# Transposing attention probabilities by DMA instead of on TensorE, in a fused attention and two-layer kernel

## The chip, the cores and the metric

The kernel runs on one core of a Trainium2 chip. The metric is the device time of one execution in microseconds, as the median of several runs. The kernel before takes 693.0 us.

The core's engines work side by side, each through its own queue of instructions in program order: TensorE (PE, with its weight loads shown apart as PEld), VectorE (DVE), ScalarE (ACT), GpSimd (POOL) and SyncE (SP), whose queue issues most of the DMA transfers here. An instruction that waits holds everything behind it on its own engine.

## The reference, cut to what matters

```python
scores = scale * np.matmul(q, k.transpose(0, 1, 3, 2))      # 4 batches, 8 heads, 576 positions, 64 wide
scores = np.where(masks, scores, -1e9)                      # window of 32, plain or dilated by 4
attn = np.exp(scores - np.max(scores, axis=-1, keepdims=True))
attn = attn / (np.sum(attn, axis=-1, keepdims=True) + 1e-09)
x = np.matmul(attn, v)                                      # then laid out as [2304 tokens, 512]
h = x @ w_in                                                # 512 -> 2048
x = (h - np.tanh(h)) @ w_out                                # 2048 -> 512
h2 = x @ w_in2                                              # 512 -> 1024, then h2 * softmax(h2), layer norm
out = ln @ w_out2                                           # 1024 -> 512
```

## The kernel before

**Units.** Attention is cut into 48 units of four blocks: each block is 96 queries against 128 keys. Eight units make the x of one group of 384 tokens; there are six groups. For each unit the scores go to PSUM (`qk_f32` for units below 20, `qk_half` twice for the others, which use split operands made by `prep_unit`). VectorE adds the mask and takes the row maximum (L337 and L340 for the split form) and writes the tile `p` of 96 x 4 x 128 float32 values. ScalarE applies the exponential in place (`sm_exp`, L348). `sm_norm` forms the reciprocal of the row sums on VectorE (L353, L354) and multiplies `p` by it on GpSimd (L356).

**The transpose.** The product with v needs the keys on the partitions. So `tr_pe` transposes the four blocks of `p` on TensorE against the identity into one PSUM tile (L363), and ScalarE copies this into the SBUF tile `pt` of 128 x 384 (L369). `pv_pe` multiplies two units' `pt` by v (L384); its evacuation writes x as a rounded part on ScalarE (L393) and a rest on VectorE (L395). PSUM tiles of attention come from the pool `a_ps`, which has two buffers. `p` has three buffers, `pt` five.

**The main stage.** Steps s = 0 to 95 are six groups by sixteen columns of the hidden layer. A step has two slots: in the first TensorE does the twelve matmuls of `mm1(s)` (L457), in the second the twelve of `mm2(s - 5)` (L484). The activation of `mm1(s)` is a chain of four: tanh on ScalarE (L465), subtraction on VectorE (L468, `sub`), rounding on ScalarE (L471, `hi`), rest on VectorE (L474, `lo`). The PSUM tiles of `mm1` have two buffers, so `mm1(s + 2)` needs `sub` of step s to be done.

**The order by hand.** `plan` hangs the work of the units of later groups into the slots. For unit u from 16 on, p = 4u - 41 is its first slot: the scores are multiplied in slots p and p + 1, the reciprocal and product come in slot p + 4, the transposes in slot p + 6, and the product with v for four units together, five slots after the transposes of the fourth one. A unit's round is thus four slots. In each slot a fixed order holds: the TensorE work, then the activation parts, the evacuations of the TensorE pieces of the slot before (`nxt`), and then the list `later` of the slot in the order of its registering.

**Loads.** All loads are issued from SP. While units 20 to 39 are worked on, the tile `qkr` of a unit is used first to bring in a piece of the second layer's weights (`sc_load`, L188), whose maximum is taken by `sc_max` (L208), and then for the unit's q and k (L179). `v` comes from L274.

**The last part.** The second layer (L748, L763 and on) uses DMA transposes already: `split_z` (L877) transposes a tile of 128 x 2048 float16 values, in two parts a and b, into `zt`.

Of the kernel before, what the change touches and what calls it, by code (L numbers as in the profile page):

```python
# [7 lines left out]
F32 = mybir.dt.float32  # L8
F32R = mybir.dt.float32r
I32 = mybir.dt.int32  # L10
F16 = mybir.dt.float16
BF16 = mybir.dt.bfloat16
U16 = mybir.dt.uint16
AF = mybir.ActivationFunctionType
ALU = mybir.AluOpType
# [9 lines left out]
NQ, NK = 96, 128  # L25
NU = 8
QC, KC = 4 * NQ, 4 * NK
# [13 lines left out]
def tile_kernel(ctx: ExitStack, tc: tile.TileContext, qk, vw, cst, w_in, w_out, w_in2, w_out2, g_ln, out):  # L41
    nc = tc.nc
    ctx.enter_context(tc.manual_schedule())

    const = ctx.enter_context(tc.tile_pool(name="const", bufs=1, side="left"))
# [12 lines left out]
    at_p = tc.alloc_tile_pool(name="at", bufs=2, side="right")  # L58
# [23 lines left out]
    ymx = const.tile([128, NG, KD], F32, name="ymx")  # L82
    ym = const.tile([128, NG], F32, name="ym")
    ysc = const.tile([128, NG // 2, 3, 3], F32, name="ysc")
    id16 = const.tile([128, 128], F16, name="id16")

# [76 lines left out]

    xt, un = {}, {}
    NFU = 20

    def new_qk(u):
        un[u] = dict(r=at_p.tile([128, QC + KC], F32, tag="qkr", name=f"qkr{u}"))  # L170

    def load_qk(u):
# [3 lines left out]
        elif u not in un:  # L176
            new_qk(u)
        n = 64 if u < NFU else 128
        nc.sync.dma_start(out=un[u]["r"][:n], in_=qk[u, :n])  # L179

    def sc_load(u, i):

        new_qk(u)
        r = un[u]["r"].bitcast(I32)
        k, q = divmod(i, 10)
        w = w_in2.rearrange("a b p n -> (a b) p n") if k else w_out2
        if q < NF2:
            nc.sync.dma_start(out=r, in_=w[q][:, 0:QC + KC])  # L188
        else:
            h = 4 * (q - NF2)  # L190
            nc.sync.dma_start(out=r[:, 0:512].rearrange("p (j n) -> p j n", j=4),
                              in_=w[h:h + 4].rearrange("j p n -> p j n")[:, :, QC + KC:])
# [84 lines left out]
    def load_unit(u):  # L277
        if u < NU * NG:
            load_qk(u)
            load_v(u)  # L280

    def prep_unit(u):
        if not NFU <= u < NU * NG:
            return []
        r = un[u]["r"]
        s = qs_p.tile([128, QC + 2 * KC], F32R, tag="qks", name=f"qks{u}")
        un[u]["s"] = s
        return [
            lambda: nc.scalar.copy(out=s[:, 0:QC + KC], in_=r),
            lambda: nc.vector.tensor_tensor(out=s[64:128, 0:QC], in0=r[64:128, 0:QC],  # L290
                                            in1=s[64:128, 0:QC].bitcast(F32), op=ALU.subtract),
            lambda: nc.vector.tensor_tensor(out=s[:, QC + KC:], in0=r[:, QC:],
                                            in1=s[:, QC:QC + KC].bitcast(F32), op=ALU.subtract),
        ]
# [7 lines left out]
    def qk_f32(u, pool, tag):  # L302

        d = un[u]
        new_p(u)
        ps = pool.tile([128, 512], F32, tag=tag, name=f"qkp{u}")[:NQ, 0:KC].rearrange("p (b k) -> p b k", b=4)
        for b in range(4):
            nc.tensor.matmul(ps[:, b], d["r"][:64, b * NQ:(b + 1) * NQ],  # L308
                             d["r"][:64, QC + b * NK:QC + (b + 1) * NK], start=True, stop=True)

        def then():
            for b in range(4):
                nc.vector.tensor_tensor_reduce(  # L313
                    out=d["p"][:, b], in0=ps[:, b], in1=masks[:, mask_of(u, b % 2)], op0=ALU.add, op1=ALU.min,
                    scale=-0.125, scalar=3.0e38, accum_out=d["nm"][:, b:b + 1])
        return then
# [28 lines left out]
    def sm_exp(u, bs=range(4)):  # L345
        d = un[u]
        for b in bs:
            nc.scalar.activation(out=d["p"][:, b], in_=d["p"][:, b], func=AF.Exp, scale=-1.0,  # L348
                                 bias=d["nm"][:, b:b + 1], accum_out=d["sm"][:, b:b + 1])

    def sm_norm(u):
        d = un[u]
        nc.vector.tensor_scalar(out=d["rs"], in0=d["sm"], scalar1=1e-9, scalar2=None, op0=ALU.add)  # L353
        nc.vector.reciprocal(out=d["rs"], in_=d["rs"])  # L354
        eng = nc.vector if u == NU - 1 else nc.gpsimd
        eng.tensor_tensor(out=d["p"], in0=d["p"],  # L356
                          in1=d["rs"].unsqueeze(2).to_broadcast([NQ, 4, NK]), op=ALU.mult)

    def tr_pe(u, pool, tag, eng="a"):
        d = un[u]  # L360
        ps = pool.tile([128, 512], F32, tag=tag, name=f"tp{u}")
        for b in range(4):
            nc.tensor.transpose(ps[:NK, b * NQ:(b + 1) * NQ], d["p"][:, b], ident[:NQ, :NQ])  # L363
        pt = at_p.tile([NK, QC], F32, tag="pt", name=f"pt{u}", bufs=5)
        d["pt"] = pt

        def then():
            if eng == "a":
                nc.scalar.copy(out=pt, in_=ps[:NK, 0:QC])  # L369
            else:  # L370
                nc.vector.tensor_copy(out=pt, in_=ps[:NK, 0:QC])
        return then

    def pv_pe(u, pool, tag):

        g, r = divmod(u, NU)
        hp = r // 2
        x = xt[g, hp] = x_ps[g % 2].tile([128, 2, G], F32R, tag=f"x{hp}", name=f"x{g}_{hp}")
        ps = pool.tile([128, 512], F32, tag=tag, name=f"pv{u}")[:, 0:G]
        for i in range(2):  # L380
            d = un.pop(u + i)
            for b in range(2):
                for h in range(2):
                    nc.tensor.matmul(ps[64 * h:64 * h + 64, (2 * i + b) * NQ:(2 * i + b + 1) * NQ], d["v"][:, b, h],  # L384
                                     d["pt"][:, (2 * h + b) * NQ:(2 * h + b + 1) * NQ], start=True, stop=True)
        sl, src = [x[:, i] for i in range(2)], ps
        if hp >= 2:
            sl = [a.rearrange("p (i r) -> p r i", r=DIL) for a in sl]
            src = ps.rearrange("p (r i) -> p r i", r=DIL)

        def then(parts="hl"):
            if "h" in parts:
                nc.scalar.copy(out=sl[0], in_=src)  # L393
            if "l" in parts:
                nc.vector.tensor_tensor(out=sl[1], in0=src, in1=sl[0].bitcast(F32), op=ALU.subtract)  # L395
        return then
# [50 lines left out]
    def at(slot, fn):  # L447
        later.setdefault(slot, []).append(fn)
# [54 lines left out]
    u0, u1 = NU, NU * NG  # L503
    preps = []

    def piece(slot, fn):
        todo.setdefault(slot, []).append(fn)

    def plan():


        ready = 0
        for u in range(u0, u1 + 2):
            p = 4 * u - 41 if u >= 2 * NU else (2, 6, 8, 12, 14, 16, 18, 20)[u - u0]
            q = p + 2 if u >= 2 * NU or u < u0 + 4 else p + 1
            if u < u1:
                at(p + 1, lambda u=u: preps.extend(prep_unit(u + 1)))
                for i in (1, 1, 2):
                    at(p + i, lambda: preps.pop(0)() if preps else None)
                if u < NFU:  # L520
                    piece(p, lambda u=u: qk_f32(u, a_ps, "at"))
                    at(p + 1, lambda u=u: sm_exp(u))
                    at(p + 2, lambda u=u: sm_norm(u))
                else:
                    piece(p, lambda u=u: qk_half(u, 0, a_ps, "at"))
                    at(p + 2, lambda u=u: sm_exp(u, (0, 1)))
                    piece(p + 1, lambda u=u: qk_half(u, 1, a_ps, "at"))
                    at(p + 3, lambda u=u: sm_exp(u, (2, 3)))
                    at(p + 4, lambda u=u: sm_norm(u))
                i = u - NFU  # L530
                if 0 <= i < 20:
                    at(p - 1, lambda u=u, i=i: sc_load(u + 2, i))
                    at(p + 1, lambda u=u, i=i: sc_max(u + 2, i))
                if i == 20:
                    at(p - 1, lambda u=u: new_qk(u + 2))
                    at(p - 1, lambda u=u: sc_rows(u + 2))
                    piece(p + 1, lambda: sc_pe(a_ps, "at"))
                at(p + 1, lambda u=u: load_unit(u + 2))
            if u0 <= u - 1 < u1:
                piece(q, lambda u=u: tr_pe(u - 1, a_ps, "at"))  # L540
            if u % 4 == 1 and u0 <= u - 5 < u1:
                for w in (u - 5, u - 3):
                    piece(q + 1, lambda w=w: pv_pe(w, a_ps, "at"))

    plan()


# [191 lines left out]
    p3 = ctx.enter_context(tc.tile_pool(name="p3", bufs=2, side="left", reuse_waits="tile"))  # L739
# [151 lines left out]
    def mm4(i, mid=None):  # L891
# [11 lines left out]
        nc.scalar.activation(out=o, in_=po, func=AF.Copy, scale=d["g"])  # L903
        nc.sync.dma_start(out=out[i * TT:(i + 1) * TT, :], in_=o)

    nc.gpsimd.tensor_copy(out=id16, in_=ident)
    y_rows(2)
    split_y(2, ("r", "s"))
# [126 lines left out]
```

## Time and profile before

| | |
|---|---|
| median of 3 runs | 693.0 us (691.96 to 693.55) |
| the profiled execution | 692.85 us, of which the trace's span is 691.1 us |
| TensorE busy | 671.4 us, 97% of the span |
| VectorE busy | 501.5 us, 73% |
| ScalarE busy | 384.3 us, 56% |
| GpSimd busy | 173.3 us, 25% |
| mean granted TensorE clock | 0.998 of full speed |

The span runs from the first to the last instruction of the trace; 1.75 us of the execution's time lie around it. Busy time is the time in which an engine has at least one instruction under way. Matmuls are pipelined: one starts before the one ahead of it has ended, so the time that a matmul costs is the distance between starts, not its own duration.

### The profile page before, as it was taken

How to read it: one execution, taken by the hardware profiler on the slowest of the kernel's cores; microseconds unless marked ns; L12 is line 12 of the kernel's file. 1: busy time of each engine (PE TensorE's matmuls, PEld its weight loads, DVE VectorE, ACT ScalarE, POOL GpSimd, SP SyncE). 2: the span in 40 equal slices, each digit the busy share in tenths (PEclk: the TensorE clock that was granted, in tenths of full speed). 3: DMA queues.
4: the chain of work that ended last, by engine and by line, in shares of the span. 5: the costliest groups of instructions: out<-in, count | busy, mean ns of one | idle time of the engine just before them, and what ended most of it. 6: DMA issues, size and time to landing. Idle time of an engine off the chain costs nothing. (4 is left out here: it accounts for less than half of the span.)

```text
span 691.1 us, 11384 instructions
## 1 busy us (share of the span) xinstructions
PE 671.4 (97%) x4010; PEld 558.3 (81%) x4010; DVE 501.5 (73%) x1251; ACT 384.3 (56%) x917; POOL 173.3 (25%) x174
## 2 busy tenths in 40 slices
PE   6988999999999999999999999999999999999997
PEld 5787999999999999999999999999964444444443
DVE  4987667468777876787767853489978888777752
ACT  5778876545554555555554543466736645555442
POOL 2312311101101110111110110246414666545410
PEclk9999999999999999999999999999999999999999
DMA  9975640233433334442322100463512464433243
GB/s 281 353 246 173 212 125 23 86 121 119 123 104 116 111 121 123 121 142 74 97 69 71 45 1 1 152 202 134 168 46 45 114 147 95 93 94 76 71 92 92
DMA packets 68009, 80.82 MB, mean 117 GB/s; under 512 B 36592, under 2 KB 52464, under 8 KB 67952
## 3 DMA queue, kind: packets, MB, share of 16 engines
q1 hardware_dynamic: 64784, 75.37, 37.6%
q10 hardware_dynamic: 3168, 4.72, 1.8%
q8 instruction: 32, 0.52, 0.3%
q14 instruction: 25, 0.20, 0.1%
HBM read 62.25 MB, written 9.44 MB: 104 GB/s over the span
## 5 line engine op out<-in xcount | busy, mean ns | idle before, releaser
L457 PE MATMUL h<-x,wi 128*128 128x384 f32 x1152 | 221.5, 342 | 1.2 <-DVE t L468 1.2
L484 PE MATMUL y<-gs,wo 128*128 128x384 f32 x1152 | 217.9, 339 | 0.0
L457 PEld LDWEIGHTS h<-x,wi 128*128 128x128 f32 x1152 | 199.4, 190 | 2.5 <-DVE t L468 1.4
L484 PEld LDWEIGHTS y<-gs,wo 128*128 128x128 f32 x1152 | 199.8, 189 | 1.8
L356 POOL TENSOR_TENSOR p<-p,rs 96x512 f32<-96x512 f32 x47 | 57.5, 1224 | 352.3 <-DVE rs L354 316.9
L474 DVE TENSOR_TENSOR gs<-t,gs 128x384 fp32r<-128x384 f32 x96 | 81.4, 848 | 24.3 <-ACT gs L471 24.2
L468 DVE TENSOR_TENSOR t<-h,t 128x384 f32<-128x384 f32 x96 | 53.0, 552 | 63.3 <-ACT t L465 63.2
L900 PE MATMUL po<-w2o_o,zt 128*128 128x512 f16 x432 | 94.9, 379 | 0.0
L465 ACT ACTIVATE t<-h 128x384 f32<-128x384 f32 x96 | 46.8, 488 | 83.3 <-PE h L457 80.0
L348 ACT ACTIVATE p<-p,nm 96x128 f32<-96x128 f32 x192 | 74.9, 392 | 21.3 <-DVE nm L313 21.0
L471 ACT CAST gs<-t 128x384 fp32r<-128x384 f32 x96 | 48.9, 509 | 63.6 <-DVE t L468 63.4
L900 PEld LDWEIGHTS <-zt 128*128 128x128 f16 x432 | 42.1, 98 | 51.1 <-DMA zt<-e 0.5
L748 PEld LDWEIGHTS <-yt 128*128 128x128 f16 x378 | 36.8, 98 | 47.0 <-issue 3.4
L823 ACT ACTIVATE e<-hn,sml 128x1024 f32<-128x1024 f32 x18 | 20.7, 1149 | 56.3 <-DVE sml L763 43.5
L748 PE MATMUL sp<-w2i_t,yt 128*128 128x512 f16 x216 | 48.6, 379 | 2.2 <-DVE u L786 2.2
L873 DVE SCALAR_TENSOR_TENSOR e<-hn,sml,e 128x1024 f16<-128x1024 f32 x18 | 25.6, 1426 | 19.6 <-ACT e L872 19.6
L748 PE MATMUL sp<-w2i_b,yt 128*128 128x512 f16 x162 | 37.9, 379 | 0.0
L308 PE MATMUL qkp<-qkr 64*96 64x128 f32 x160 | 29.5, 339 | 7.3 <-DMA qkr<-in_qk_dram 5.5
L348 ACT ACTIVATION_READ_ACCUMULATOR p<-p,nm 96x1 f32 x192 | 36.2, 188 | 0.0
L308 PEld LDWEIGHTS qkp<-qkr 64*96 64x96 f32 x160 | 24.1, 205 | 11.8 <-DMA qkr<-in_qk_dram 5.9
L395 DVE TENSOR_TENSOR x<-pv,x 128x384 fp32r<-128x384 f32 x24 | 16.2, 697 | 19.8 <-ACT x L393 19.4
L363 PE MATMUL tp<-cst_sb,p 96*128 96x96 f32 x192 | 27.0, 268 | 3.4 <-POOL p L356 2.4
(111 smaller groups left out, 826.2 us busy)
## 6 DMA issues: line engine op xcount, KB each, us to landing
qkr<-in_qk_dram SPq DMA_DIRECT2D x28, 448.0 KB, 3.4
raw_wi<-in_w_in_dram SPq DMA_DIRECT2D x16, 511.8 KB, 7.2
raw_wo<-in_w_out_dram SPq DMA_DIRECT2D x16, 511.8 KB, 7.1
v<-in_vw_dram SPq DMA_DIRECT2D x48, 128.0 KB, 3.4
y_dr<-ys ACTq DMA_DIRECT2D x6, 768.0 KB, 3.9
yr<-y_dr SPq DMA_DIRECT2D x9, 512.0 KB, 4.5
out_dram<-o SPq DMA_DIRECT2D x18, 256.0 KB, 2.9
qkr<-in_qk_dram SPq DMA_DIRECT2D x20, 224.0 KB, 5.2
```

The costliest lines, as they stand in the source:

```text
L308: nc.tensor.matmul(ps[:, b], d["r"][:64, b * NQ:(b + 1) * NQ], d["r"][:64, QC + b * NK:QC + (b + 1) * NK], start=True, stop=True)
L348: nc.scalar.activation(out=d["p"][:, b], in_=d["p"][:, b], func=AF.Exp, scale=-1.0, bias=d["nm"][:, b:b + 1], accum_out=d["sm"][:, b:b + 1])
L356: eng.tensor_tensor(out=d["p"], in0=d["p"], in1=d["rs"].unsqueeze(2).to_broadcast([NQ, 4, NK]), op=ALU.mult)
L363: nc.tensor.transpose(ps[:NK, b * NQ:(b + 1) * NQ], d["p"][:, b], ident[:NQ, :NQ])
L457: nc.tensor.matmul(ps, w[:, a, k * 128:(k + 1) * 128], xt[g, k][:, b], start=(n == 0), stop=(n == 3 * KD - 1))
L465: nc.scalar.activation(out=t, in_=ps, func=AF.Tanh)
L468: nc.vector.tensor_tensor(out=t, in0=ps, in1=t, op=ALU.subtract)
L471: nc.scalar.copy(out=gs[:, 0], in_=t)
L474: nc.vector.tensor_tensor(out=gs[:, 1], in0=t, in1=gs[:, 0].bitcast(F32), op=ALU.subtract)
L484: nc.tensor.matmul(yb[g][m], wo[c][:, a, m * 128:(m + 1) * 128], gs[:, b], start=(c == 0 and i == 0), stop=(c == NF - 1 and i == 2))
L748: nc.tensor.matmul(ps, y[:, a, blk, kk], w2i[w, kk][:, b], start=first and q == 0, stop=q == 5, skip_group_check=not first)
L900: nc.tensor.matmul(po, z[:, a, j], w2o[j][:, b], start=(q == 0), stop=(q == 3 * NF2 - 1))
```

## The change

For units 16 to 47 (`DT` = 16 is the first), TensorE does not transpose `p` any more.

- `sm_norm` divides the row sum by 2^14 in the instruction that adds 1e-9, so that `p` comes out 2^14 times as large.
- `p_new` takes a further tile of the tag `p` (three buffers, as before, now for two tiles a unit) and views it as float16.
- `p_hi`, in slot p + 5, copies `p` on ScalarE into the first half of it as float16; `p_lo`, in slot p + 6, writes `p` less that copy into the second half on VectorE, and issues a DMA transpose of the 96 x 1024 float16 values from SP into the new tile `ptt` (two buffers).
- `p_sum`, in slot p + 9, adds the two transposed parts on VectorE into `pt`, which has four buffers now.
- The evacuation in `pv_pe` takes the factor 2^14 out again: the ScalarE copy gets a scale, the VectorE subtraction becomes a multiply and subtract.
- The float16 identity `id16` moves from the constants into the pool of the last part, so its memory is reserved later.

```diff
+    DT = 2 * NU
...
     def sm_norm(u):
         d = un[u]
-        nc.vector.tensor_scalar(out=d["rs"], in0=d["sm"], scalar1=1e-9, scalar2=None, op0=ALU.add)
+        nc.vector.tensor_scalar(out=d["rs"], in0=d["sm"], scalar1=1e-9, scalar2=2.0 ** -14 if u >= DT else 1.0,
+                                op0=ALU.add, op1=ALU.mult)
...
+    def p_new(u):
+        un[u]["ab"] = at_p.tile([NQ, 4, NK], F32, tag="p", name=f"pab{u}", bufs=3).bitcast(F16).rearrange(
+            "p b (a k) -> p (b a k)", a=2)
+
+    def p_hi(u):
+        d = un[u]
+        nc.scalar.copy(out=d["ab"][:, 0:4 * NK], in_=d["p"].rearrange("p b k -> p (b k)"))
+
+    def p_lo(u):
+        d = un[u]
+        ab = d["ab"]
+        nc.vector.tensor_tensor(out=ab[:, 4 * NK:], in0=d["p"].rearrange("p b k -> p (b k)"), in1=ab[:, 0:4 * NK],
+                                op=ALU.subtract)
+        d["tt"] = at_p.tile([NK, 2, 4, NQ], F16, tag="ptt", name=f"ptt{u}")
+        nc.sync.dma_start_transpose(out=d["tt"].rearrange("p a b q -> p (a b) q"), in_=ab)
+
+    def p_sum(u):
+        d = un[u]
+        d["pt"] = at_p.tile([NK, QC], F32, tag="pt", name=f"pt{u}", bufs=4)
+        nc.vector.tensor_tensor(out=d["pt"].rearrange("p (b q) -> p b q", b=4), in0=d["tt"][:, 0], in1=d["tt"][:, 1],
+                                op=ALU.add)
...
-        pt = at_p.tile([NK, QC], F32, tag="pt", name=f"pt{u}", bufs=5)
+        pt = at_p.tile([NK, QC], F32, tag="pt", name=f"pt{u}", bufs=4)
...
         def then(parts="hl"):
+            if g * NU >= DT:
+                nc.scalar.activation(out=sl[0], in_=src, func=AF.Copy, scale=2.0 ** -14)
+                nc.vector.scalar_tensor_tensor(out=sl[1], in0=src, scalar=2.0 ** -14, in1=sl[0].bitcast(F32),
+                                               op0=ALU.mult, op1=ALU.subtract)
+                return
...
-            if u0 <= u - 1 < u1:
+            if DT <= u < u1:
+                for i, fn in ((3, p_new), (5, p_hi), (6, p_lo), (9, p_sum)):
+                    at(p + i, lambda u=u, fn=fn: fn(u))
+            if u0 <= u - 1 < min(u1, DT):
                 piece(q, lambda u=u: tr_pe(u - 1, a_ps, "at"))
```

## Rows read from the trace of the kernel before

**Rows 1.** The page, busy time, share of the span and instructions of each engine.
```profile
PE 671.4 (97%) x4010; PEld 558.3 (81%) x4010; DVE 501.5 (73%) x1251; ACT 384.3 (56%) x917; POOL 173.3 (25%) x174
```

**Rows 2.** Windows: stretch, its length, busy us of each engine, clock, DMA share, GB/s.
```profile
100.00:420.00 320.00, 320.00 (x2127) 313.93 (x2126) 228.56 (x658) 171.76 (x484) 35.27 (x34) 1.00 0.29 91
138.58:414.99 276.41, 276.41 (x1842) 272.17 (x1842) 203.46 (x585) 147.00 (x418) 30.24 (x30) 1.00 0.31 97
...
300.00:320.00 20.00, 20.00 (x145) 19.52 (x144) 16.98 (x49) 12.01 (x37) 2.08 (x2) 1.00 0.42 135
```

**Rows 3.** Timeline of TensorE, end of attention: start us, us, instruction.
```profile
410.82 2.24 PE L457 MATMUL h<-x,wi 128*128 128x384 f32 x12
412.90 2.24 PE L484 MATMUL y<-gs,wo 128*128 128x384 f32 x12
414.99 0.49 PE L363 MATMUL tp<-cst_sb,p 96*128 96x96 f32 x4
...
417.43 2.24 PE L484 MATMUL y<-gs,wo 128*128 128x384 f32 x12
```

**Rows 4.** Groups of instructions by line: count, busy us, mean ns of one, idle before.
```profile
L356 DVE TENSOR_TENSOR p<-p,rs 96x512 f32<-96x512 f32 x1 | 0.7, 689 | 0.0
...
L290 DVE TENSOR_TENSOR qks<-qkr,qks 64x384 fp32r<-64x384 f32 x28 | 15.6, 556 | 0.9
...
L369 ACT COPY pt<-tp 128x384 f32<-128x384 f32 x48 | 22.8, 474 | 5.0 <-PE tp L363 4.8
...
L289 ACT CAST qks<-qkr 128x896 fp32r<-128x896 f32 x28 | 26.2, 937 | 0.0
...
L363 PE MATMUL tp<-cst_sb,p 96*128 96x96 f32 x192 | 27.0, 268 | 3.4 <-POOL p L356 2.4 <-DVE p L356 0.9
```

**Rows 5.** Timeline of all engines, one round: start us, us, instruction, idle before.
```profile
251.34 0.50 PE L363 MATMUL tp<-cst_sb,p 96*128 96x96 f32 x4
...
251.96 0.33 SPq L188 DMA_DIRECT2D qkr<-in_w_in_dram  x1
...
254.57 0.56 DVE L468 TENSOR_TENSOR t<-h,t 128x384 f32<-128x384 f32 x1 [2.13 <-ACT t L465]
...
255.58 1.04 POOL L356 TENSOR_TENSOR p<-p,rs 96x512 f32<-96x512 f32 x1 [8.14 <-DVE rs L354]
255.58 0.94 ACT L289 CAST qks<-qkr 128x896 fp32r<-128x896 f32 x1
...
255.71 1.32 DVE L474 TENSOR_TENSOR gs<-t,gs 128x384 fp32r<-128x384 f32 x1 [0.30 <-ACT gs L471]
...
256.10 2.25 PE L457 MATMUL h<-x,wi 128*128 128x384 f32 x12
256.95 0.41 DVE L337 TENSOR_TENSOR p<-qkp,cst_sb 96x256 f32<-96x256 f32 x1
...
257.93 0.56 DVE L290 TENSOR_TENSOR qks<-qkr,qks 64x384 fp32r<-64x384 f32 x1
...
258.45 0.49 ACT L465 ACTIVATE t<-h 128x384 f32<-128x384 f32 x1 [1.94 <-PE h L457]
258.52 0.62 DVE L208 TENSOR_REDUCE mx<-qkr 128x1 f32<-128x448 bf16 x1
...
259.93 0.55 DVE L468 TENSOR_TENSOR t<-h,t 128x384 f32<-128x384 f32 x1
...
260.52 0.50 PE L363 MATMUL tp<-cst_sb,p 96*128 96x96 f32 x4
```

**Rows 6.** Timeline of TensorE, transposes of unit 19.
```profile
145.32 0.49 PE L363 MATMUL tp<-cst_sb,p 96*128 96x96 f32 x4
```

**Rows 7.** Instructions of tile zt: duration ns, min/median/max, and their landing.
```profile
L877 SPq DMA_TRANSPOSE zt<-e x16: 1696/1906/3652, 528.5 to 676.6; - x16
...
DMA to landing us min/median/max: 4.2/4.3/5.9
```

**Rows 8.** DMA from 528 to 534 us: busy tenths in 40 slices.
```profile
DMA  0000000000005999999999999999810000000000
```

More of the change, by code (lines that the diff above doesn't have):

```diff
@@ L84, in tile_kernel @@
     ysc = const.tile([128, NG // 2, 3, 3], F32, name="ysc")
-    id16 = const.tile([128, 128], F16, name="id16")
     wq, wld, wa, wf, wh = [], [], [], [], []
@@ L904, in mm4 @@
         nc.sync.dma_start(out=out[i * TT:(i + 1) * TT, :], in_=o)
+    id16 = p3.tile([128, 128], F16, name="id16", bufs=1)
     nc.gpsimd.tensor_copy(out=id16, in_=ident)
```

## The prediction

> **What bounds the kernel now.** I read the page first: TensorE is busy 97% of the span, VectorE 73% [rows 1]. Busy time alone doesn't prove a bound, so the windows come next. From 100 to 420 us, which holds all the work that is changed (the first changed unit's scores come at slot 23, just before 100 us), TensorE is busy 320.00 of 320 us at a granted clock of 1.00, VectorE 228.56, ScalarE 171.76, and the DMA engines 29% [rows 2]. The reader should see an engine without a gap beside one with 29% to spare. The timeline then shows that matmuls follow each other at their own pace: the twelve of one slot begin 2.08 us after the twelve of the slot before [rows 3], and nothing waits in between. So in this stage a matmul that goes away shortens the kernel by its pitch, as long as no other engine becomes the slowest. What comes behind 420 us depends on the stage's end and shifts with it.
>
> **What the change takes from TensorE.** It removes the four transposes of each of 32 units, 128 instructions. The groups give 268 ns for one [rows 4], which would make 34 us, but that counts overlapped time. The timeline has the price: from one `mm2` slot's start to the next `mm1` to the next `mm2`, slots without transposes take 2.08 us (410.82 to 412.90), and from the transposes at 414.99 past the following `mm1` to the next `mm2` at 417.43 it is 2.44 us [rows 3]. The difference, 0.36 us, is what four transposes cost with the switch of shapes. 32 x 0.36 = 11.4 us (unrounded 0.355).
>
> A round of four slots is 9.18 us now, from the transposes at 251.34 to those at 260.52 [rows 5], and would be 8.83. With the products with v and the group ends the average round is (414.99 - 145.32) / 28 = 9.63 us, from unit 19's transposes to unit 47's [rows 3, 6]; it would be 9.28.
>
> **What it adds to VectorE.** `p_lo` is a two-operand instruction on 96 x 512; the same shape on VectorE took 689 ns. `p_sum` has 384 elements a partition; L290 with as many took 556 ns [rows 4]. Together 1.25 us a unit. Neither operand mix (float16 with float32) is in the trace; the upper end is that each also meets GpSimd's product as `lo` does, which takes 1.32 us beside it [rows 5] against L290's 0.56, so 0.76 more each and 2.77 in all. The lower end is that either costs what its row shows and no more. I take 1.25, since GpSimd's one product a unit already slows one VectorE instruction and the new ones come later in the round. VectorE's demand was 203.46 of 276.41 us [rows 2], 7.09 per average round; it becomes 8.34 of 9.28, or 90%. It fits, with less reserve: around a group's end, where `y_max` comes in, VectorE is at 16.98 of 20 [rows 2], and 2.6 more makes 19.6 against 19.3 that the shorter rounds leave. That overrun is a queue, not yet a stall: the `sub` that ends at 255.13 is needed only by the `mm1` two steps on, behind the transposes at 260.52, over 5 us later [rows 5]. I allow 1 us in all for such places; bounds 0 and 5 us (eight dense rounds of 0.6). The factor in the evacuation leaves the number of instructions as it is: costed at nothing, hidden by VectorE's reserve, and at most a tenth of a microsecond in 16 places if not.
>
> **What it adds to ScalarE.** The copy `pt` of 474 ns goes, `p_hi` with 512 elements comes; between 474 ns for 384 and 937 for 896 [rows 4] that is about 0.59, so 0.12 more a unit, 4 us in all, on an engine busy 171.76 of 320 [rows 2]. More important is its place: `p_hi` waits for GpSimd's product, and behind it in ScalarE's queue stand the cast `qks` (L289) and the next tanh. In the round shown the product ends at 256.62; p_hi to 257.3, cast to 258.2. The tanh starts at 258.45 because its matmuls end only then [rows 5], so it isn't delayed. VectorE wants the cast for L290 at 257.93, but `p_sum` now stands ahead of it and moves that to 258.5. Cost nothing; if the product takes longer, VectorE waits for that in its 10% reserve.
>
> **What it adds to SP and the DMA engines.** 32 transposes of 96 x 1024 float16, 192 KB each, against the 512 KB of `zt`. The latter holds SP for 1.9 us and lands 4.3 us (4.2 to 5.9) after its issue [rows 7]. In one such transfer the DMA engines start 1.8 us into the window, 1.3 us after the issue at 528.5, and run for about 2.5 [rows 7, 8]. At three eighths of the bytes that is 0.95, and 1.3 + 0.95 + 0.5 for the end gives 2.8 us. Bounds: 2.8 and zt's longest, 5.9. I take 3, as the DMA engines are 29% busy; loads issued a slot earlier are mostly through. On SP, the next `sc_load` (251.96) is queued behind `p_lo` and the transpose, some 1 to 2 us later. It is read at 258.52 [rows 5]; with 4 us of transfer it still arrives in time. `load_qk` and `load_v` have a round to spare. POOL's queue gets no more instructions.
>
> **The new loop.** `p` still has three buffers, but a unit takes two. Unit u + 2's first VectorE write (L337) goes into unit u's float16 tile, so it must wait for unit u's DMA transpose. The loop of a round is: `p_lo`, landing, L337, and on VectorE everything up to the next `sub` and the next `p_lo`. From L337 at 256.95 to the end of `sub` at 260.48 is 3.53 us [rows 5]; with `p_sum` and `p_lo` 4.78. A landing of L us makes a loop of L + 4.78: 7.8 at L = 3, under the 8.83 of the shortest round. At zt's 4.3 it is 9.1, still under the average 9.28, the products with v giving the time back. `id16` and the smaller number of `pt` buffers cost nothing: the identity is first wanted in the last part, and `pt` of a unit is written after the product with v that frees it.
>
> A rule that speaks against the change: the Trainium skill, VectorE: DVE Perf Modes, section The three transpose paths, gives 390 ns for a 128 x 128 bf16 transpose on TensorE and 1309 ns by DMA. By these prices of the Trainium skill, an estimate, eight tiles one after another would land in 10.5 us and every round would last 15 us. The trace disagrees for tiles in one transfer: sixteen land together in 4.3 us [rows 7].
>
> **The sum.** The profiled execution is 692.85 us, its span 691.1. 692.85 - 11.4 + 1 = 682.5. The median shown, 693.0, is 0.15 above it, so 682.6.
>
> **The rivals.**
> *VectorE becomes the bound.* At the upper price of 2.77 us its demand is 9.86 a round against 9.28: 32 x 0.58 = 18.6 us back, 700 us. From 2.19 us on the gain shrinks, at 2.54 it is gone. For it: 90% busy in an engine that works in order, with new waits on ScalarE and DMA. Against it: it still waits 2.13 us for a tanh in the round shown [rows 5]. Halfway, with an extra wait of 1.2 us a round, the time is about 690.
> *The transposes land late (slower than before).* The place is L337's wait for the buffer of `p`. The loop equals today's average round of 9.63 at L = 4.85; above that the kernel is slower. At 5.9 it is 10.68, 1.05 us a round more, 32 x 1.05 = 34: 727 us. For it: zt reached 5.9, and loads share the queue. Against it: three eighths of the bytes. The prices of the Trainium skill (VectorE: DVE Perf Modes, The three transpose paths) would put the kernel in this case.
> *The cost of the transposes was hidden anyway.* If something else gave the pace, the time would stay at 693. Against it: 0.36 us more in every slot with transposes, without an idle TensorE [rows 2, 3].
>
> **How the numbers follow.** My forecast (680.5 to 686) gets 0.67; VectorE partly in the way (686 to 691.5) 0.12; no change 0.04; VectorE fully the bound 0.05; late transposes 0.12. The likeliest is 682.6. The range of 680.5 (11.4 taken and a little more) to 692 holds the first two and part of the third, 8 in 10; the late case would lie far outside. Differences below 0.2%, 1.4 us, can't be told from none. Faster: 0.79; same: 0.04; slower: 0.17.
>
> **What would show it.** In the changed profile: 128 fewer TensorE instructions, and 64 transposes left at L363; rounds of about 8.83 us without the product with v; `p_lo` near 0.69 and `p_sum` near 0.56 us, 32 each; VectorE near 268 of 309 us in the stage; DMA transposes of `ptt` landing in about 3 us; and no idle time of VectorE at the first write of `p`. Wrong, it would be: TensorE idle before `mm1` with `sub` as the releaser, VectorE idle behind the DMA of `ptt`, or landings of more than 4.5 us.

## The result and the profile after

The changed kernel takes 684.88 us, the median of four runs (683.13 to 686.35), against 692.93 us before (four runs, 691.96 to 693.55): a ratio of 0.9884 with a 95% interval of 0.9857 to 0.9911. It is 1.2% faster: the direction is as forecast, the time is inside the range of 680.5 to 692 and 2.3 us above the likeliest value of 682.6. The profiled execution took 683.13 us, its span 681.3.

The page's busy times answer to [rows 1]: 128 instructions of TensorE are gone, 64 of VectorE are new (`p_lo` and `p_sum`).

```profile
PE 661.0 (97%) x3882; PEld 547.9 (80%) x3882; DVE 532.6 (78%) x1315; ACT 386.3 (57%) x917; POOL 174.5 (26%) x174
```

The window that answers to [rows 2], with the columns told there, ends at 410 us now, since the work behind it moved forward by 9.7 us:

```profile
100.00:410.00 310.00, 309.99 (x2007) 304.03 (x2006) 260.80 (x723) 174.74 (x486) 36.37 (x34) 1.00 0.43 114
```

TensorE still has no gap, VectorE rose from 71% to 84%, and the DMA share from 0.29 to 0.43. So the bound of the stage is what it was. Rounds without the product with v are read from the timeline of TensorE, at the first scores (L328) of three units in a row:

```profile
206.55 0.40 PE L328 MATMUL qkp<-qks 128*96 128x256 f32 x2
...
215.36 0.40 PE L328 MATMUL qkp<-qks 128*96 128x256 f32 x2
...
224.17 0.40 PE L328 MATMUL qkp<-qks 128*96 128x256 f32 x2
```

They are 8.81 us apart; before it was 9.18 [rows 5], and 8.83 was forecast. The new instructions, by the tile that holds the two float16 parts (durations in ns as min/median/max, then first and last start):

```profile
L366 ACT CAST pab<-p x32: 612/619/623, 110.8 to 402.3; 96x512 f16<-96x512 f32 x32
L371 DVE TENSOR_TENSOR pab<-p,pab x32: 676/678/679, 115.8 to 404.8; 96x512 f16<-96x512 f32 x32
L374 SPq DMA_TRANSPOSE ptt<-pab x32: 1212/1213/2224, 116.6 to 405.5; - x32
its engine sat idle before it (us, times) until:
  POOL p L357: 23.4, 24
  DMA ptt<-pab: 8.0, 4
...
DMA to landing us min/median/max: 2.8/2.9/4.8
```

L366 is `p_hi`, L371 `p_lo`, L374 the transpose; `p_sum` (L379) has a median of 550 ns. The reader should see two things: a landing of 2.9 us, and that the instruction that waits for landings is `p_hi` on ScalarE, in four places (`p_sum` waits once, for 0.2 us).

**The stage gave 11.1 us, and 8.1 arrived.** From the first scores of slot 23 to the last product with v, the timelines of TensorE give 99.27 to 425.85 us before and 100.69 to 416.13 after: 326.58 against 315.44, or 11.1 us less. But the stage began 1.4 us later than before. This profiled run is the fastest of the four, 9.7 us under the profiled run before, where the medians are 8.1 apart; the profile of a run nearer the median, below, shows a start 3.15 us late. What makes it late stands some 16 us ahead of it, in work that the change was not meant to touch. The timeline of all engines of the changed kernel:

```profile
81.86 0.88 PE L407 MATMUL pv<-pt,v 128*64 128x96 f32 x16
...
82.45 0.48 ACT L392 COPY pt<-tp 128x384 f32<-128x384 f32 x1 [1.64 <-PE pv L407]
...
82.98 0.88 PE L407 MATMUL pv<-pt,v 128*64 128x96 f32 x16 [0.25 <-ACT pt L392]
...
85.48 1.58 PE L308 MATMUL qkp<-qkr 64*96 64x128 f32 x8 [1.61 <-DVE x L423]
```

The copy of transposed probabilities into `pt` waits 1.64 us for the product with v, the product falls into two halves, and the next scores wait 1.61 us for its evacuation. That looks like a lack of `pt` buffers, of which the change took one. The first experiments test it.

### The profile page after: what moved, and what is told of

It reads as the page before. It is cut to its first block, busy times and chain, and to the rows that moved or that the text cites. A ratio compares the mean times of both kernels' runs of the same rounds, so it can differ in the third digit from the quotient of the medians.

```text
span 681.3 us, 11184 instructions
## 1 busy us (share of the span) xinstructions
PE 661.0 (97%) x3882; PEld 547.9 (80%) x3882; DVE 532.6 (78%) x1315; ACT 386.3 (57%) x917; POOL 174.5 (26%) x174
## 5 line engine op out<-in xcount | busy, mean ns | idle before, releaser
L485 PE MATMUL h<-x,wi 128*128 128x384 f32 x1152 | 218.7, 339 | 0.8 <-DVE t L496 0.8
L366 ACT CAST pab<-p 96x512 f16<-96x512 f32 x32 | 19.8, 619 | 31.4 <-POOL p L357 23.4
L313 DVE CUSTOM_DVE_ANT_0 p<-qkp,cst_sb 96x128 f32<-96x128 f32 x80 | 18.3, 281 | 14.9 <-PE qkp L308 8.2
```

Of the source, the lines that this page charges most:

```text
L485: nc.tensor.matmul(ps, w[:, a, k * 128:(k + 1) * 128], xt[g, k][:, b], start=(n == 0), stop=(n == 3 * KD - 1))
```

## The experiments

The runs were taken in three sets, and the kernel before was timed again in each: 692.76, 692.13 and 692.95 us. Ratios are to these. A difference in microseconds between runs of different sets carries their spread, 0.8 us. In the diffs `...` stands for lines left out.

**The changed kernel again.** No edit; it is the base for the other runs of its set.

> The changed kernel once more, as the yardstick for the other runs on this chip. Every theory: 683 to 686 us, 8 us under the kernel before. The trace should again show rounds of 8.82 us in the main stage, and a stall of TensorE near 85 us.

Measured: 684.71 us, ratio 0.9887 (0.9869 to 0.9904). The result stands. Its profiled run began slot 23 at 102.42 us and ended the last product with v at 417.71, so the stage took 315.29 us and started 3.15 us late: 11.3 gained, 3.15 lost, which is the 8.1 us that the medians differ by. The first profile began 1.7 us earlier than this one because TensorE did not fall to the lower clock at 56 to 66 us in it, as it did in this run and in the profiled run before (last section).

**The fifth `pt` buffer given back.** `ptt` gets one buffer in exchange, to fit the memory.

```diff
-        d["tt"] = at_p.tile([NK, 2, 4, NQ], F16, tag="ptt", name=f"ptt{u}")
+        d["tt"] = at_p.tile([NK, 2, 4, NQ], F16, tag="ptt", name=f"ptt{u}", bufs=1)
...
-        d["pt"] = at_p.tile([NK, QC], F32, tag="pt", name=f"pt{u}", bufs=4)
+        d["pt"] = at_p.tile([NK, QC], F32, tag="pt", name=f"pt{u}", bufs=5)
...
-        pt = at_p.tile([NK, QC], F32, tag="pt", name=f"pt{u}", bufs=4)
+        pt = at_p.tile([NK, QC], F32, tag="pt", name=f"pt{u}", bufs=5)
```

> The tile pt has five buffers again, and the tile ptt one in place of two. Theory: the fourth buffer's loss makes ScalarE wait near 82 us (its copy of unit 12's transposes waits 1.64 us for the product with v that frees the buffer), TensorE then stalls 1.9 us near 83 to 85 us, where the kernel before stalled 0.5, and sometimes runs at half the clock behind it; so this kernel is 1.4 to 3 us faster than the changed one, at 682 to 683.5, and the wait at the copy is gone. Rival: the early stretch varies from run to run anyway and the missing microseconds lie in the main stage; then it takes the same time as the changed kernel, within 0.7 us.

Measured: 681.43 us (681.28 to 681.63), ratio 0.9838 (0.9825 to 0.9852), 3.3 us below the changed kernel of the same set, a little more than expected, and 11.3 below the kernel before. The timeline at the same place:

```profile
82.45 0.47 ACT L392 COPY pt<-tp 128x384 f32<-128x384 f32 x1
...
83.59 1.54 PE L407 MATMUL pv<-pt,v 128*64 128x96 f32 x32
...
85.64 1.11 PE L308 MATMUL qkp<-qkr 64*96 64x128 f32 x8 [0.51 <-DVE x L423]
```

The copy no longer waits, the product is whole, and slot 23's scores come at 99.30 us, as before the change (99.27). So the missing buffer caused the loss. It is the version to keep of all that was run, with the two at its side that differ from it by less than the intervals tell (below).

**The kernel before with four `pt` buffers.** The other half of the same test: the buffer taken from a kernel that has nothing else of the change.

```diff
-        pt = at_p.tile([NK, QC], F32, tag="pt", name=f"pt{u}", bufs=5)
+        pt = at_p.tile([NK, QC], F32, tag="pt", name=f"pt{u}", bufs=4)
```

> The kernel before with four buffers of pt in place of five, nothing else. Theory of the buffer: 1.4 to 3 us slower than before, 694.4 to 696, with ScalarE's wait near 82 us; in the main stage a further wait could come, since there the fifth unit's copy stands one slot behind the product with v. Rival: within 0.7 us of before.

Measured: 698.84 us, ratio 1.0097 (1.0081 to 1.0112), 6.1 us more than before: more than either expectation. Its waits, as total, times and longest, over the span:

```profile
ACT pt L369 <- PE pv L384: 17.4, 9, 3.1
```

In the kernel before the transposes of a fifth unit come four slots after those of the fourth, and the product with v for the four comes five slots after. So the fifth copy finds the four buffers full, nine times here. In this profile slot 23 begins 3.0 us late, from the first of the nine, and the stage is 4.0 us longer, from the other eight. In the changed kernel `p_sum` writes `pt` only in slot p + 9, three slots later, and that is behind the product; only one copy by `tr_pe`, ahead of unit 16, is caught. That is why the buffer costs the changed kernel 3.3 us and not 6.

**The transposes kept beside the new path.** All of the change stays, and TensorE also transposes `p` of units 16 to 47 into a PSUM tile that nothing reads.

```diff
...
+            elif DT <= u - 1 < u1:
+                piece(q, lambda u=u: tr_idle(u - 1, a_ps, "at"))
```

> The changed kernel, in which TensorE also does the four transposes of units 16 to 47 as before, into a PSUM tile that nothing reads. Theory: the gain is the pitch of these matmuls, 0.355 us a unit, so 11.4 us come back: 695 to 697, a little above before, since the pt buffer's cost stays; rounds of 9.18 us. Rival: a part of the gain comes from the PSUM tile and the ScalarE copy that went away; then less than 9 us come back.

Measured: 696.08 us, ratio 1.005 (1.0034 to 1.0067), 11.4 us over the changed kernel. Its timeline of TensorE has the old round back, 9.19 us between the scores of two units:

```profile
143.41 0.40 PE L328 MATMUL qkp<-qks 128*96 128x256 f32 x2
...
148.07 0.49 PE L401 MATMUL tx<-cst_sb,p 96*128 96x96 f32 x4
...
152.60 0.40 PE L328 MATMUL qkp<-qks 128*96 128x256 f32 x2
```

The price of the pitch, 32 x 0.355 = 11.4 us, is shown in both directions, and the rival, that a part of the gain came from the PSUM tile and the copy, falls.

**The added work left out.** On the version with five buffers, nothing of the new path runs, and the products with v of units 16 to 47 read an old `pt`.

```diff
...
-                for i, fn in ((3, p_new), (5, p_hi), (6, p_lo), (9, p_sum)):
-                    at(p + i, lambda u=u, fn=fn: fn(u))
+                at(p + 9, lambda u=u: old_pt(u))
```

> On the kernel with five pt buffers (681.4 us): units 16 to 47 do none of the transposing; p_new, p_hi, p_lo, the DMA transpose and p_sum are left out, and pv_pe multiplies the transposed probabilities of unit 15 in their place, so the attention of those units is left out of the result. Theory: all the added work is hidden behind TensorE; the same time within 0.7 us. Rival: the added work costs something in places, above all at the group ends; then 1 us or more faster, under 680.4.

Measured: 681.34 us, ratio 0.9845 (0.9822 to 0.9869), the same as with the added work. On the timelines the way from the first split scores to the last product with v is 274.49 us without it and 275.03 with it. So all of the added work costs 0.5 us by the two profiles (the medians can't tell that from nothing), though it occupies VectorE for 28.5 us more between 140 and 400 us. The windows without it:

```profile
140.00:400.00 260.00, 260.00 (x1695) 256.76 (x1694) 200.03 (x575) 132.79 (x385) 30.19 (x30) 1.00 0.32 103
```

and with it, on the version with five buffers:

```profile
140.00:400.00 260.00, 260.00 (x1691) 256.09 (x1691) 228.57 (x637) 146.26 (x413) 28.35 (x28) 1.00 0.45 124
```

**VectorE's additions twice.** How much reserve is left? On the version with five buffers `p_lo` and `p_sum` each run twice (1.23 us more a unit). The diffs of this run and the next show the lines put in; each stands for the single instruction it repeats.

```diff
+        for _ in range(2):
+            nc.vector.tensor_tensor(out=ab[:, 4 * NK:], in0=d["p"].rearrange("p b k -> p (b k)"), in1=ab[:, 0:4 * NK],
+                                    op=ALU.subtract)
...
+        for _ in range(2):
+            nc.vector.tensor_tensor(out=d["pt"].rearrange("p (b q) -> p b q", b=4), in0=d["tt"][:, 0], in1=d["tt"][:, 1],
+                                    op=ALU.add)
```

> On the kernel with five pt buffers (681.4 us): p_lo and p_sum each run twice, which puts 0.68 + 0.55 = 1.23 us more on VectorE in each of 32 units. VectorE was busy 260 of 310 us in the main stage; 39 more makes 299, or 96%. Theory of the prediction (from the demand a round, the gain is gone when 2.54 us are added, and 2.46 are added here): 9.55 us of demand against rounds of 9.28, so 8 to 10 us slower, 689 to 692. Rival: the queue on VectorE may lag by several microseconds before TensorE feels it, and its demand still fits the stage; then less than 3 us slower, at most 684.5.

Measured: 703.57 us, ratio 1.0166 (1.015 to 1.0181), 22 us more than with five buffers. Both expectations missed. The window of the stage and one row of its waits:

```profile
100.00:430.00 330.00, 313.58 (x1996) 301.59 (x1995) 296.74 (x783) 171.95 (x484) 36.38 (x34) 1.00 0.39 107
```

```profile
PE qkp L328 <- DVE qks L292: 9.4, 14, 1.6
```

TensorE stands still 16 of 330 us, while VectorE is busy 90% of it and not 100%. The average round, over the 15 from 148.44 to 298.87 us, is 10.03 us.

**Only `p_sum` twice** (0.55 us more a unit), a smaller dose on the same version.

```diff
+        for _ in range(2):
+            nc.vector.tensor_tensor(out=d["pt"].rearrange("p (b q) -> p b q", b=4), in0=d["tt"][:, 0], in1=d["tt"][:, 1],
+                                    op=ALU.add)
```

> On the kernel with five pt buffers (681.4 us): only p_sum runs twice, 0.55 us more on VectorE a unit. With both p_lo and p_sum twice, 1.23 us more made 22 us, 0.7 a unit, so VectorE's order has a reserve of about 0.5 us a round. Theory of a reserve of 0.5 us: 0 to 3 us slower, 681.4 to 684.5. Rival: the cost rises in proportion from the first tenth; then 0.55 / 1.23 of 22, 10 us slower, 691.

Measured: 687.71 us, ratio 0.9924 (0.9896 to 0.9952), 6.3 us more than with five buffers: between the expectations. Where most of it is lost, in TensorE's timeline:

```profile
224.54 0.45 PE L328 MATMUL qkp<-qks 128*96 128x256 f32 x2 [0.82 <-DVE qks L292]
...
300.13 0.44 PE L328 MATMUL qkp<-qks 128*96 128x256 f32 x2 [0.90 <-DVE qks L292]
...
332.46 0.68 PE L227 MATMUL scp<-cst_sb,wsc 128*128 128x128 f32 x4 [0.99 <-DVE nm L340]
...
395.26 0.68 PE L227 MATMUL ysp<-cst_sb,ym 128*128 128x128 f32 x4 [1.21 <-DVE ym L249]
```

Of the plain rounds many still take 8.81 to 8.87 us (253.15 to 261.96, 177.28 to 186.15). The stalls stand where VectorE has the extra work of a group's end (ahead of 224.54 it copies two tiles of y out of PSUM, 1.01 us from 220.45) or of the scales (`scp`, `ysp`). Between the two doses 0.68 us of added work a unit cost 15.9 us, which is 0.73 us of time for each us of work. If the cost rises in a straight line, which two doses can't show, the first 0.28 us a round are free.

**`p_lo` behind the operand that is waited for.** Since TensorE waited for `qks` of L292, just behind `p_lo` on VectorE, `p_lo` was registered later in the list of the same slot, behind L292: once with the additions twice, once on the version with five buffers.

```diff
-                for i, fn in ((3, p_new), (5, p_hi), (6, p_lo), (9, p_sum)):
+                for i, fn in ((3, p_new), (5, p_hi), (9, p_sum)):
                     at(p + i, lambda u=u, fn=fn: fn(u))
+            if DT <= u - 1 < u1:
+                at(p + 2, lambda u=u: p_lo(u - 1))
```

> The kernel with p_lo and p_sum run twice (703.6 us), in which p_lo stands behind L292 in VectorE's queue and not ahead of it; the amount of work is the same. Theory: what TensorE waited for there is L292, which makes the split operand for the next unit's scores, and 1.36 us less stand ahead of it now; the time falls to 690 or below. Rival: VectorE's whole queue sets the round, in whatever order; then it stays at 700 or above.

Measured: 703.25 us, ratio 1.0149 (1.0119 to 1.0179), no different from 703.57. The theory that the order before L292 was the cause falls: TensorE's waits at L292 fell from 9.4 us in all to 2.9 (one of 1.33 us at 258.36 remained), and others grew (2.34 us before `scp` at 343.37, 1.31 before it with the old order), so that between 130 and 415 us it stands still for 16.9 us, against 16.4. That fits the rival, that VectorE's whole queue sets the pace. It doesn't show it, because the edit did a second thing: with `p_lo` later the landing is later too, and `p_hi` waits for it 18 times in that window, where it waited 5 times for 10.3 us.

```profile
ACT pab L366 <- DMA ptt<-pab: 28.2, 18, 3.2
```

> The kernel with five pt buffers (681.4 us) with p_lo behind L292 as in the run beside it, nothing twice. Every theory: the same within 0.7 us, since L292 was done some 2 us before its reader in the ordinary rounds; at most 0.5 us is to be had at the group ends.

Measured: 681.17 us, ratio 0.9827 (0.98 to 0.9855): the same as with five buffers. Here too `p_hi` waits 18 times for landings, 27.0 us, and nothing is lost by it.

**The DMA transpose twice and three times** into the same tile, on the version with five buffers, to bring about the late landing. The diff is that of twice; for three times it is `range(3)`.

```diff
-        nc.sync.dma_start_transpose(out=d["tt"].rearrange("p a b q -> p (a b) q"), in_=ab)
+        for _ in range(2):
+            nc.sync.dma_start_transpose(out=d["tt"].rearrange("p a b q -> p (a b) q"), in_=ab)
```

> On the kernel with five pt buffers (681.4 us): each DMA transpose is issued twice in a row into the same tile, so that the second lands about 1.3 us later, 4.2 us after p_lo. Theory of the loop (landing, p_hi of the next unit, and from there to p_lo 5.1 us in all): 9.3 us against average rounds of 9.28 and short ones of 8.82; 0 to 4 us slower, 681.4 to 685.5, ScalarE waiting for ptt in most rounds. Rival: the loop has more slack than counted, and the time stays within 0.7 us.

> On the kernel with five pt buffers (681.4 us): each DMA transpose is issued three times in a row, landing about 5.5 us after p_lo. Theory of the loop: 5.5 + 5.1 = 10.6 us a round against 9.28 on average, so 32 x 1.3 = 42 us slower, 715 to 730, slower than the kernel before. Rival: a late transpose only delays work off TensorE's path, within the slack of the slots; then less than 10 us slower.

Measured: 734.12 us, ratio 1.0612 (1.0591 to 1.0633), and 817.25, ratio 1.1797 (1.177 to 1.1825): 52.7 and 135.8 us more than with five buffers. All the ranges expected were missed, and those of the theory were far too small: the second transfer waits for the first one's landing, as both write one tile and the program puts a wait between them, so that two land after 5.8 us and not 4.2. SP is held for 4.05 us by two, where one takes 1.21. One round with two transposes, all engines:

```profile
251.31 0.68 DVE L371 TENSOR_TENSOR pab<-p,pab 96x512 f16<-96x512 f32 x1
...
252.06 4.05 SPq L375 DMA_TRANSPOSE ptt<-pab  x2
...
257.80 0.62 ACT L366 CAST pab<-p 96x512 f16<-96x512 f32 x1 [2.27 <-DMA ptt<-pab]
258.32 0.94 ACT L289 CAST qks<-qkr 128x896 fp32r<-128x896 f32 x1
259.29 0.56 DVE L290 TENSOR_TENSOR qks<-qkr,qks 64x384 fp32r<-64x384 f32 x1 [1.01 <-ACT qks L289]
...
260.93 0.41 DVE L337 TENSOR_TENSOR p<-qkp,cst_sb 96x256 f32<-96x256 f32 x1
...
262.27 0.68 DVE L371 TENSOR_TENSOR pab<-p,pab 96x512 f16<-96x512 f32 x1
```

Its waits in the stage:

```profile
ACT pab L366 <- DMA ptt<-pab: 96.6, 28, 5.5
...
DVE pt L380 <- DMA ptt<-pab: 34.7, 22, 3.2
```

From one `p_lo` to the next it is 10.96 us: 0.68 for itself, 5.81 to the landing, and 4.47 from `p_hi` to the next `p_lo`. So the loop is L + 5.15. Against the average round of 9.28 that is 1.68 us a unit, 54 us in all, and 52.7 were measured. With three the landing is about 8.7 us, an estimate of three times 2.9, and the loop 13.85: 146 us worked out, 135.8 measured. Most of the difference is in the counting: from the first `p_lo` (115.9) to the last (542.7) there are 31 distances of 13.77 us, against 9.32 with five buffers (114.4 to 403.2), which makes 138. Worked out from the run with two, the landing that the kernel bears on average is 9.28 - 5.15 = 4.1 us; no run here has landings between 2.9 and 5.8 us in most rounds, so that edge is not tested.

**The transpose in two halves** of 96 x 512, each into its own half of `ptt`, on the version with five buffers.

```diff
-        nc.sync.dma_start_transpose(out=d["tt"].rearrange("p a b q -> p (a b) q"), in_=ab)
+        for a in range(2):
+            nc.sync.dma_start_transpose(out=d["tt"][:, a], in_=ab[:, a * 4 * NK:(a + 1) * 4 * NK])
```

> On the kernel with five pt buffers (681.4 us): the DMA transpose is issued as two of 96 x 512, one for each part, into different halves of ptt, so that neither waits for the other. Landing of the second perhaps 3.5 to 4 us after p_lo in place of 2.9. Theory of the loop (landing + 5.1 us, average round 9.28, so free up to a landing of 4.2): the same time within 0.7 us. Rival: every microsecond of landing costs, 32 x 0.6 to 1.1, so 19 us or more slower.

Measured: 680.93 us, ratio 0.9823 (0.9791 to 0.9854), the same as with five buffers. Here the two don't wait for each other: SP is held for 2.48 us by both, and the second is issued before the first has landed. Each lands in nearly the time that the whole took:

```profile
DMA to landing us min/median/max: 2.3/2.5/6.4
```

But the time says nothing on the edge of 4.1 us. The first half holds only what `p_hi` wrote, so it doesn't wait for `p_lo` and goes ahead of it:

```profile
246.59 2.48 SPq L375 DMA_TRANSPOSE ptt<-pab  x2
246.91 0.68 DVE L371 TENSOR_TENSOR pab<-p,pab 96x512 f16<-96x512 f32 x1
...
251.00 0.62 ACT L366 CAST pab<-p 96x512 f16<-96x512 f32 x1 [0.98 <-POOL p L357]
```

Two issues of 1.19 us put the second at about 247.9, and 2.5 us later, at 250.4, it has landed: 2.8 us after the end of `p_lo`, as early as the whole transpose. The landing of 3.5 to 4 us that was expected didn't come about, so neither the theory nor the rival was tested.

## Why the prediction was right, and where it was not

**The gain from TensorE: right.** 11.4 us were forecast from the pitch of 0.355 us; the transposes put back cost 11.4 us, and the version with five buffers is 11.3 us faster than the kernel before, with the 0.5 us that the added work costs already taken off. The 268 ns of [rows 4] for each transpose would have made it three times as much.

**VectorE: the costs right, the reserve wrong.** `p_lo` was taken at 689 ns and took 678, `p_sum` at 556 and took 550. The allowance of 1 us for dense places measures 0.5. VectorE's busy time rose less than forecast, to 260.80 of 310 us and not 268 of 309, in part because instructions in a row overlap: `p_lo` starts at 257.29 and lasts 0.68 us, and L292 behind it starts at 257.89. But the step that VectorE "fits, with less reserve", with a gain that shrinks from 2.19 us of added work on and is gone at 2.54, mis-sized the reserve. 1.23 + 0.55 = 1.78 us already cost 6.3 us, and by the straight line between the two doses, an estimate, the 11.3 us would be gone at 1.23 + 0.77 = 2.0 us. The reserve was worked out as 9.28 less 8.34 us of busy time; but VectorE also waits for ScalarE, and a part of that stays however much work is added. Between 130 and 415 us the wait for the tanh shrinks from 15.5 us with five buffers to 2.8 with the additions twice; the wait of `lo` for `hi` stays, 10.4 us in 31 places and 9.2 in 29. The rival "VectorE becomes the bound" was nearer than its price made it look.

**ScalarE: right.** 0.59 us was the estimate for `p_hi`, 0.619 is measured. The queue behind it went as worked out. In the changed kernel's timeline the product ends at 253.04, `p_hi` and the cast follow, and the tanh waits for its matmuls alone, 0.28 us:

```profile
252.00 1.04 POOL L357 TENSOR_TENSOR p<-p,rs 96x512 f32<-96x512 f32 x1 [7.28 <-DVE rs L355]
...
253.07 0.62 ACT L366 CAST pab<-p 96x512 f16<-96x512 f32 x1 [0.97 <-POOL p L357]
...
253.60 0.94 ACT L289 CAST qks<-qkr 128x896 fp32r<-128x896 f32 x1
...
254.24 0.55 DVE L379 TENSOR_TENSOR pt<-ptt 128x384 f32<-128x384 f16 x1
...
254.81 0.49 ACT L493 ACTIVATE t<-h 128x384 f32<-128x384 f32 x1 [0.28 <-PE h L485]
254.83 0.56 DVE L290 TENSOR_TENSOR qks<-qkr,qks 64x384 fp32r<-64x384 f32 x1
```

**The landing: right.** 3 us was taken, 2.9 measured. Single landings took up to 4.8, beyond the 4.5 named as a sign of being wrong, but TensorE has no gap in the stage. The price by DMA of the Trainium skill (VectorE: DVE Perf Modes, The three transpose paths), by which, as an estimate, eight tiles would land in 10.5 us, can't be multiplied by eight for tiles in one transfer: they land in 2.9 us, and the measurement decides.

**The new loop: it exists, at another place.** The prediction had it wait at L337 on VectorE for the buffer of `p`, with a loop of L + 4.78. It had the three buffers of the tag go round in turn. In the program as built, the float16 tiles of units 16 to 46 all have one and the same buffer, and the `p` tiles of the later units take turns in the other two. The traces agree: no row shows a wait at L337 for a landing. What waits for the landing is `p_hi` of the next unit on ScalarE, and the loop goes through `p_hi`, the cast behind it, L290, the scores' mask and maximum, `sub` and `p_lo`, and is L + 5.15. At 2.9 us it takes 8.05 of the 8.82 and is free, as forecast; that two different paths are nearly as long is luck. By the average round it is bound at 4.1 us, where 9.28 - 4.78 = 4.5 followed from the forecast. The late-transposes rival was right in that late landings make the kernel slower, through `p_hi` and not L337, and didn't come about, since the landings were short. One of the four waits in the changed kernel, in its timeline, stands where a landing took 4.55 us:

```profile
148.73 1.21 SPq L374 DMA_TRANSPOSE ptt<-pab  x1
...
153.28 0.62 ACT L366 CAST pab<-p 96x512 f16<-96x512 f32 x1 [2.07 <-DMA ptt<-pab]
```

**The buffers: the step that failed.** "`id16` and the smaller number of `pt` buffers cost nothing ... `pt` of a unit is written after the product with v that frees it". That is so for `p_sum`, which the sentence thought of. It left out the last units that `tr_pe` still transposes. The plan puts the transposes of unit 12 in slot 17 and the product that frees its buffer, that of units 8 and 9, in slot 18, so with four buffers the copy of unit 12 waits. This term was put at nothing and costs 3.3 us; about 1.4 of it is the longer stall and up to 1.7 the lower clock behind it (last section). Half a microsecond of the allowance wasn't needed; that leaves 2.8 against the 2.3 by which the forecast was off, which the spread of the medians covers. `id16` was not tested by itself, but with its move the version with five buffers has the whole gain.

## What to carry to other kernels

A matmul removed from a stream without gaps gives back its pitch, so read it from the distance of starts with and without it, and not from its duration. Where a change takes a buffer from a tile, follow the order of writes and reads for each producer of that tile, the units at the edge of the change too. Time in which an engine that works in order is idle is not all reserve: here VectorE was busy 228.57 of 260 us, 1.1 us short of full in each round, and by the line of two doses about 0.3 us of that could be used for nothing. Doubling the new work on the chip shows how near the edge is. And when a test is to move one time, read in its trace that this time did move: the transpose in halves left the landing where it was.

## What the hardware showed that was not expected

**A short stall of TensorE can cost a second time.** Two windows of the changed kernel, around a place further ahead and around the stall at 83.9 to 85.5 us; the last three columns are granted clock, DMA share and GB/s:

```profile
56.00:66.00 10.00, 7.76 (x48) 7.05 (x47) 8.05 (x26) 8.74 (x23) 3.82 (x2) 1.00 0.68 202
84.00:94.00 10.00, 8.52 (x45) 7.81 (x46) 4.45 (x17) 5.40 (x17) 1.91 (x1) 0.83 0.33 91
```

and of the version with five buffers:

```profile
56.00:66.00 10.00, 7.79 (x39) 7.47 (x38) 7.88 (x24) 8.66 (x23) 3.82 (x2) 0.83 0.51 163
84.00:94.00 10.00, 9.49 (x81) 8.73 (x78) 6.53 (x28) 6.65 (x22) 3.42 (x2) 1.00 0.46 135
```

A mean of 0.83 over 10 us is 3.4 us at the lower level of 1.2 GHz and the rest at 2.4, so up to 1.7 us of TensorE's work is lost. Behind the stall of 1.6 us the clock fell, and without it (0.5 us there) it didn't: in the window of 84 to 94 us all four profiles of kernels with four `pt` buffers show 0.83 or less, and all ten with five show 1.00. The spell at 56 to 66 us, around idle time that both kernels have, is there in some executions and missing in others: the kernel before shows 0.83 there, the changed kernel run again 0.83 in both windows, its first profile in the second alone. Those two profiled runs of the changed kernel took 684.71 and 683.13 us, so the spell makes part of the spread. Why it comes and goes, no run here tells.

**DMA transposes overlap when nothing in the program holds them apart.** Two into one tile, where the program makes the second wait, land after 5.8 us; two into its halves, with half of the bytes each, take about 3.8 us from the first issue to the last landing.
